# One group of zeros a pass in place of two, masks ahead of pooled scores, and a product moved into the pooled scores' buffer

## The chip, the cores and the metric

The kernel runs on one core of one Trainium2 chip. Its time is the device time of one execution in microseconds; the kernel before took 652.89 us as the median of three runs (650.90 to 655.39). One execution of it was profiled.

## The reference

Attention over 2 batches of 8 heads, 576 tokens, head size 64, followed by two feed-forward networks. The attention has two parts that are added: a local one, in which a token sees the three tokens on either side, and a pooled one over means of four tokens.

```python
def sm_attn(qq, kk, vv):
    s = scale * np.matmul(qq, kk.transpose(0, 1, 3, 2))
    s = s - np.max(s, axis=-1, keepdims=True)
    a = np.exp(s)
    a = a / (np.sum(a, axis=-1, keepdims=True) + 1e-09)
    return np.matmul(a, vv)
q_d = q.reshape(B, H, Sd, factor, D).mean(axis=3)      # k_d, v_d likewise, factor = 4
out_up = np.repeat(sm_attn(q_d, k_d, v_d), factor, axis=2)
mask = np.abs(pos[:, None] - pos[None, :]) < factor
scores = np.where(mask, scale * np.matmul(q, k.transpose(0, 1, 3, 2)), -1000000000.0)
# softmax of scores, times v: out_local
return (out_up + out_local).astype(np.float32)
```

The result x (1152 tokens of 512 numbers) goes through h = x w_in, g = h clip(h + 3, 0, 6) / 6, g w_out, and then through four experts, max(x w1, 0) w2, weighted by normalised probabilities and added.

## The kernel before

The attention runs in units of two heads (one batch, one pair of heads): eight units, numbered by `units`. A loop over t (lines 1116 to 1177, a pass below) works on three units at once: pass t makes the scores of unit t, transposes the probabilities of unit t - 1 and multiplies those of unit t - 2 with the values. Passes 8 and 9 only finish, and in between they already work on the first pieces of the next network (`pieces`, `first`, products L382 to L384). After the loop comes that network, then the experts.

In every pass from 2 to 7 TensorE gets, in this order: pooled scores (`pooled_scores`, L728) with four products of zeros ahead of them (`idle_products`, L605, 128 x 128 by 128 x 512, bf16), masks (`masks`, L652) and scores (`scores`, L665), transposes (`turn`, L712) with four more zeros ahead, values (`values`, L802) and pooled values (L813, in the same function), and pooled transposes (`pooled_turn`, L782). The products of zeros go into the buffer that the next real products overwrite. Pass 1 has the first four zeros only, pass 8 has neither.

The order on all five engines is that of the program's text; waits follow from the use of tiles. In a pass VectorE takes: maximum of the pooled scores (L741) and its scaling (L743), maximum of the scores (L682) and their subtraction (L683), the low half of an earlier result (L843), sums and reciprocals (L764 to L696), the adding up of both attentions (`xf`, L827), and one step of the conversion of the first network's weights (`convert`: L245, L255, L267, L276, L234). In passes 5 and 6 it also adds rows by fours for the pooled values of batch 1 (`add_four`, L452). ScalarE takes the exponentials (L753, L689), copies the transposes out (L719, L720, L790), copies pooled values (L821), writes the high half (L835) and steps of the conversion. GpSimd multiplies by the reciprocals (L769, L698) and sums q and k by fours for later units (`sums`, L452). Loads are issued by SyncE; some are held back by a one-element memset of VectorE (`hold`, L189).

Results of TensorE go into pairs of PSUM banks. `banks()` hands out three pairs in turn: each call takes the one that was handed out three calls earlier, and its first write waits for the last reader of that one. `banks(True)` hands out a fourth pair, on its own, for the values. `pool_last_v` (L485) multiplies the last 67 rows of v so that the last sixteen pooled keys of batch 1 come out; in the kernel before it uses the fourth pair at the end of pass 5's scores, and ScalarE copies the result out (L488).

Of the kernel before, what the change touches and what calls it, by code (L numbers as in the profile page):

```python
# [30 lines left out]
B, H, S, D = 2, 8, 576, 64  # L31
NHP = H // 2
# [31 lines left out]
NU = B * NHP  # L64
PK = S // FACTOR
KC = PK // 2


KR = ((80, 64), (P, PK - P))
# [56 lines left out]
def model(ctx: ExitStack, tc: tile.TileContext, qT, kT, v, dp, w_in, w_out, w1, w2, out):  # L126
# [15 lines left out]
    def banks(last=False):  # L142

        pool = psum["last"] if last and "last" in psum else psum["pair"]
        return pool.tile([P, 2, 512], F32, tag="pair", name="pair")
# [19 lines left out]
    def give(slot):  # L165
        unused[slot[1]] += 1
# [312 lines left out]
        for kc in range(2):  # L479
            nc.scalar.activation(out=pooled_v(0, kc), in_=pool[: KR[0][kc], kc, :], func=AF.Copy)  # L480

    def pool_last_v():

        to = banks(True)[: KR[1][1], 0, :]
        nc.tensor.matmul(  # L485
            to, last_fours, v_slots[1][NP - 1][0][:LAST_ROWS, :DM], start=True, stop=True
        )
        nc.scalar.activation(out=pooled_v(1, 1), in_=to, func=AF.Copy)  # L488
# [69 lines left out]
    for j in range(1, NJ):  # L558
        n = NI if j < 2 else NI - 1
# [43 lines left out]
    def idle_products(ps, count):  # L603
        for n in range(count):
            nc.tensor.matmul(ps[:, n % 2, :], zeros[:, :P], zeros, start=True, stop=True)  # L605

    class Unit:
# [91 lines left out]
                out=ex, in0=ex, in1=rec.unsqueeze(3).to_broadcast([QT, 2, NI, W]), op=ALU.mult  # L699
            )  # L700

        def turn(self, idle):

            tr = banks()
            idle_products(tr, idle)

            for p in range(NP):
                for h in range(2):
                    at = (2 * p + h) * HQ
                    for b in range(2 if p < NP - 1 else 1):  # L710
                        rows = slice(b * HQ, (b + 1) * HQ)
                        nc.tensor.transpose(  # L712
                            tr[:, b, at : at + HQ],
                            self.ex[rows, h, 2 * p : 2 * p + 2, :].rearrange("q r w -> q (r w)"),
                            ident[rows, rows],
                        )
            n = 2 * NP * HQ
            self.aT = att.tile([P, n + n - 2 * HQ], F32, tag="aT", name="aT", bufs=2)
            nc.scalar.activation(out=self.aT[:, :n], in_=tr[:, 0, :n], func=AF.Copy)  # L719
            nc.scalar.activation(out=self.aT[:, n:], in_=tr[:, 1, : n - 2 * HQ], func=AF.Copy)  # L720

        def pooled_scores(self, idle):
            self.sd = banks()
            idle_products(self.sd, idle)
            for qh in range(2):
                for h in range(2):
                    d = slice(h * D, (h + 1) * D)
                    nc.tensor.matmul(  # L728
                        self.sd[:KC, h, qh * PK : (qh + 1) * PK],
                        self.qd[d, qh * KC : (qh + 1) * KC],  # L730
                        self.kd[d],
# [41 lines left out]
                op=ALU.mult,  # L773
            )

        def pooled_turn(self):
            tr = banks()
            for h in range(2):
                for qh in range(2):
                    for kc in range(2):  # L780
                        c0 = kc * PK + qh * KC
                        nc.tensor.transpose(  # L782
                            tr[: self.kr[kc], h, c0 : c0 + KC],
                            self.exd[:, 2 * h + qh, kc * self.kr[0] : kc * self.kr[0] + self.kr[kc]],
                            ident[:KC, :KC],
                        )
            self.aTd = att.tile([P, 2, 2 * PK], F32, tag="aTd", name="aTd", bufs=2)
            for kc, n in enumerate(self.kr):
                part = slice(kc * PK, (kc + 1) * PK)
                nc.scalar.activation(out=self.aTd[:n, :, part], in_=tr[:n, :, part], func=AF.Copy)  # L790

        def values(self):
            b, hp = self.b, self.hp
            pv = banks(True)
            col = [(hp * 2 + h) * D for h in range(2)]
            for p, j, r in sorted((i // 2, j, i % 2) for i, j, _ in WINDOWS):
                c0 = p * QT + j * QB
                keys = slice(r * WP, r * WP + W)
                for h in range(2):
                    at = j * DM + col[h]  # L800
                    to = (j // 2 * 2 * NP + 2 * p + h) * HQ + j % 2 * QB
                    nc.tensor.matmul(  # L802
                        pv[h * D : (h + 1) * D, r, c0 : c0 + QB],
                        v_slots[b][p][0][keys, at : at + D],
                        self.aT[keys, to : to + QB],
                        start=True,
                        stop=True,
                    )
            toks = slice(b * S, (b + 1) * S)
            hi, lo = x[:, 0, hp, toks], x[:, 1, hp, toks]  # L810
            for kc in range(2):
                for h in range(2):
                    nc.tensor.matmul(  # L813
                        pv[h * D : (h + 1) * D, 0, NI * HQ : NI * HQ + PK],
                        pooled_v(b, kc)[:, col[h] : col[h] + D],
                        self.aTd[: self.kr[kc], h, kc * PK : (kc + 1) * PK],
                        start=(kc == 0),
                        stop=(kc == 1),
                    )
            pd = att.tile([P, 2 * KR[0][0]], F32, tag="pd", name="pd", bufs=1)  # L820
            nc.scalar.activation(out=pd[:, :PK], in_=pv[:, 0, NI * HQ : NI * HQ + PK], func=AF.Copy)  # L821
            xf = att.tile([P, NI * QT], F32, tag="xf", name="xf", bufs=2)
            self.xf = xf[:, :S]
            nj = 2 * QB // FACTOR
            for r in range(2):
                n = NI - r
                nc.vector.tensor_tensor(  # L827
                    out=xf.rearrange("p (a r j f) -> p a r j f", r=2, j=nj, f=FACTOR)[:, :n, r],
                    in0=pv[:, r, : n * 2 * QB].rearrange("p (a j f) -> p a j f", j=nj, f=FACTOR),
                    in1=pd.rearrange("p (a r j) -> p a r j", r=2, j=nj)[:, :n, r]  # L830
                    .unsqueeze(3)
                    .to_broadcast([P, n, nj, FACTOR]),
                    op=ALU.add,
                )
            nc.scalar.activation(out=hi, in_=self.xf, func=AF.Copy)  # L835
            self.hl = hi, lo
            if hp == NHP - 1:
                for s in v_slots[b]:
                    give(s)
# [238 lines left out]
    units = [Unit(u) for u in range(NU)]  # L1078
# [37 lines left out]
    for t in range(NU + 2):  # L1116
        if t == NU:
            psum.pop("last").release()
            psum["few"] = ctx.enter_context(
                tc.tile_pool(name="few", bufs=2, space=PSUM, side="right")  # L1120
            )
        if t < NU:
            n = units[t]
            if t == 0:
                n.masks(IDLE)
                n.scores()
                n.pooled_scores(0)
                n.less_max()
                units[1].sums()
                n.pooled_softmax()  # L1130
                n.normalise()
            else:
                n.pooled_scores(4)
                n.masks(0)
                n.scores()
                n.pooled_softmax()
                if t == 1:
                    units[0].pooled_normalise()
                    make_last_fours()
                    units[2].sums()  # L1140
                    load_qk(2)
                load_next(t)
                n.less_max()
        if t == NHP + 1:
            pool_last_v()
        if t == NHP + 2:
            add_four(1)
        if 2 < t < NU + 1:
            units[t - 3].low()
        if 0 < t < NU:  # L1150
            n.pooled_normalise()
            n.normalise()
            load_next(t)
        if 0 < t < NU - 2:
            units[t + 2].sums()
        if t == NU:
            pieces(1, banks()[:, 0, :TC])
        if t >= NU:
            units[t - 2].values()
        if t > NU:  # L1160
            pieces(1)
            units[t - 3].low()
            units[t - 2].low()
        if 1 <= t <= NU:
            units[t - 1].turn(0 if t in (1, NU) else 4)
        if 2 <= t < NU:
            units[t - 2].values()
        if t == 1:
            pool_v(8)
        if 1 <= t <= NU:  # L1170
            units[t - 1].pooled_turn()
        if t == NHP + 1:
            add_four(0)
        convert(3 if t >= NU else 2 if t == 3 else 1 if t > 3 else 0)
        load_next(t)
        if t >= NU:
            pieces(1)
# [130 lines left out]
    for r in range(NR):  # L1308
        h = [
            work["pool"].tile([P, 2, 2, NT], F32R, tag="h", name="h", bufs=2) for _ in range(2)  # L1310
        ]
# [85 lines left out]
```

## Time and profile before

| | |
|---|---|
| median of three runs | 652.89 us (650.90 to 655.39) |
| span of the profiled execution | 651.4 us (no time of its own is given beside it) |
| TensorE products busy | 642.8 us, 99% of the span |
| VectorE, ScalarE, GpSimd busy | 64%, 39%, 15% of the span |
| passes 2 to 7 | 19.64 to 66.03 us |

Times are microseconds from the start of the span. Shares over the whole span say little of the passes, which are its first tenth; the stages there are read from timelines and windows. An engine's row in the timeline tells its start, its length, the line, and in brackets how long the engine stood idle before it and what ended that.

### The profile page before, as it was taken

Reading aid. Unit: us, or ns where it says so; the run is one execution under the profiler, and the core shown is the slowest. Engines: PE = TensorE matmul, PEld = TensorE weight load, DVE = VectorE, ACT = ScalarE, POOL = GpSimd, SP = SyncE. Lnnn points to the kernel's source line nnn. Section 1 sums busy time; section 2 is a strip of 40 time slices with the busy share of each in tenths; the row PEclk is TensorE's granted clock in tenths of the full one; section 3 lists DMA queues with packets and bytes.
Section 4 is the critical chain, followed back from the end, with each engine's and each line's share of the span. In section 5 each row is a group of like instructions: output and inputs, shape, how many; then the busy total and the mean of one; then the engine's idle time right before and its main releaser. Section 6 shows DMA issues by size and latency. Waiting matters only on the chain.

```text
span 651.4 us, 11939 instructions
## 1 busy us (share of the span) xinstructions
PE 642.8 (99%) x4909; PEld 581.5 (89%) x4909; DVE 417.8 (64%) x848; ACT 252.7 (39%) x590; POOL 95.8 (15%) x141
## 2 busy tenths in 40 slices
PE   7999999999999999999999999999999999999997
PEld 3556899999999999998898998998998998988986
DVE  6578799962596228595575665665665765765742
ACT  5566576542464235352232233233241341331310
POOL 4753100000000035200201201201201201201000
PEclk9988999999999999999999999999999999999999
DMA  8754424500330110300110110110110210300012
GB/s 260 243 175 148 187 84 138 186 1 1 130 130 0 65 65 1 130 2 1 65 65 0 66 65 0 65 65 2 64 65 1 87 45 0 130 1 1 2 49 97
DMA packets 13368, 46.97 MB, mean 72 GB/s; under 512 B 1385, under 2 KB 4457, under 8 KB 9602
## 3 DMA queue, kind: packets, MB, share of 16 engines
q1 hardware_dynamic: 13314, 46.21, 21.0%
q8 instruction: 38, 0.62, 0.4%
q14 instruction: 16, 0.13, 0.1%
HBM read 43.85 MB, written 2.36 MB: 71 GB/s over the span
## 4 chain that ended last, share of the span: by engine, by line
PE 95%; DMA 2%; DVE 1%; SPq 1%; ACT 0%; issue 0%; POOL 0%; ACTq 0%; POOLq 0%
PE bank L994 27%; PE bank L382 10%; PE bank L383 10%; PE bank L384 10%; PE bank L1273 10%; PE bank L1274 10%; PE bank L1275 10%; PE pair L802 2%; PE pair L605 2%; DMA slot<-in_qT_dram 1%; PE pair L813 1%; DMA slot<-in_v_dram 1%; PE pair L728 1%; PE pair L782 1%; PE pair L665 1%; PE pair L712 0%
## 5 line engine op out<-in xcount | busy, mean ns | idle before, releaser
L994 PEld LDWEIGHTS bank<-xop,slot 128*128 128x128 f32 x1344 | 180.0, 188 | 1.2
L994 PE MATMUL bank<-xop,slot 128*128 128x288 f32 x1344 | 180.8, 295 | 0.0
L1274 PE MATMUL bank<-slot,h 128*128 128x512 f32 x288 | 112.2, 390 | 0.0
L1273 PE MATMUL bank<-slot,h 128*128 128x512 f32 x288 | 112.1, 389 | 0.0
L1275 PE MATMUL bank<-slot,h 128*128 128x512 f32 x288 | 112.1, 389 | 0.0
L1281 DVE SCALAR_TENSOR_TENSOR slot<-bank,pr,slot 128x512 f32<-128x512 f32 x63 | 47.3, 750 | 80.7 <-PE bank L1275 80.7
L452 POOL TENSOR_TENSOR st<-slot 128x256 f32<-128x256 f32 x16 | 13.8, 862 | 462.0 <-DMA slot<-in_w_dram 232.0
L384 PE MATMUL bank<-h,slot 128*128 128x384 f32 x192 | 64.7, 337 | 0.0
L382 PE MATMUL bank<-h,slot 128*128 128x384 f32 x192 | 64.7, 337 | 0.0
L383 PE MATMUL bank<-h,slot 128*128 128x384 f32 x192 | 64.7, 337 | 0.0
L1275 PEld LDWEIGHTS bank<-slot,h 128*128 128x128 f32 x288 | 54.1, 188 | 11.4
L1273 PEld LDWEIGHTS bank<-slot,h 128*128 128x128 f32 x288 | 54.1, 188 | 10.7
L1274 PEld LDWEIGHTS bank<-slot,h 128*128 128x128 f32 x288 | 54.1, 188 | 10.6
L382 PE MATMUL bank<-x,slot 128*128 128x384 f32 x188 | 63.2, 336 | 0.0
L384 PE MATMUL bank<-x,slot 128*128 128x384 f32 x188 | 63.0, 335 | 0.0
L383 PE MATMUL bank<-x,slot 128*128 128x384 f32 x188 | 63.0, 335 | 0.0
L452 DVE TENSOR_TENSOR u<-bank,u 128x288 f32<-128x288 f32 x96 | 43.6, 454 | 20.4 <-PE bank L994 20.0
L1023 ACT ACTIVATE h<-c 128x288 fp32r<-128x288 f32 x64 | 27.7, 445 | 70.8 <-DVE c L452 70.8
L312 ACT ACTIVATE slot<-st 128x512 fp32r<-128x512 f32 x32 | 19.2, 624 | 63.0 <-POOL st L306 63.0
L883 DVE TENSOR_TENSOR h<-slot,h 128x384 fp32r<-128x384 f32 x48 | 27.0, 576 | 24.1 <-ACT h L882 24.0
L874 ACT ACTIVATE t<-bank,half__145 128x384 f32<-128x384 f32 x47 | 27.0, 580 | 38.7 <-PE bank L384 38.5
L875 DVE SCALAR_TENSOR_TENSOR slot<-t,bank 128x384 f32<-128x384 f32 x47 | 25.7, 551 | 24.3 <-ACT t L874 24.1
(121 smaller groups left out, 925.4 us busy)
## 6 DMA issues: line engine op xcount, KB each, us to landing
slot<-in_w_dram SPq DMA_DIRECT2D x16, 1024.0 KB, 4.9
slot<-in_w_out_dram SPq DMA_DIRECT2D x8, 1024.0 KB, 5.0
slot<-in_w_in_dram SPq DMA_DIRECT2D x5, 1024.0 KB, 5.9
slot<-in_v_dram SPq DMA_DIRECT2D x8, 512.0 KB, 5.5
slot<-in_w_in_dram SPq DMA_DIRECT2D x6, 512.0 KB, 4.4
out_dram<-slot SPq DMA_DIRECT2D x9, 256.0 KB, 2.0
slot<-in_kT_dram SPq DMA_DIRECT2D x3, 576.0 KB, 4.4
slot<-in_qT_dram SPq DMA_DIRECT2D x6, 288.0 KB, 5.0
```

The costliest lines, as they stand in the source:

```text
L382: nc.tensor.matmul(ps, wh, xh, start=first, stop=False)
L383: nc.tensor.matmul(ps, wh, xl, start=False, stop=False)
L384: nc.tensor.matmul(ps, wl, xh, start=False, stop=last)
L452: eng.tensor_tensor(out=out, in0=a, in1=b, op=ALU.add)
L874: nc.scalar.activation(out=t, in_=ps, func=AF.Relu, bias=half_, scale=1.0 / (6.0 * UP))
L883: nc.vector.tensor_tensor(out=g[:, 1, :], in0=u, in1=r32(g[:, 0, :]), op=ALU.subtract)
L994: nc.tensor.matmul(ps, a[:, i, k], b[:, j, k], start=start and k == 0 and n == 0, stop=stop and k == 1 and n == 2, skip_group_check=True,)
L1023: nc.scalar.activation(out=self.h[:, 0, i, j], in_=of, func=AF.Relu)
L1273: nc.tensor.matmul(ps, hh, w[:, 0], start=(f == 0), stop=False)
L1274: nc.tensor.matmul(ps, hh, w[:, 1], start=False, stop=False)
L1275: nc.tensor.matmul(ps, hl, w[:, 0], start=False, stop=(f == NF - 1))
L1281: nc.vector.scalar_tensor_tensor(out=to, in0=ps, scalar=share, in1=to, op0=ALU.mult, op1=ALU.add)
```

## The change

Masks and pooled scores change places at the head of a pass, and the four zeros ahead of the pooled scores and the four ahead of the transposes go. In passes 2 to 7, four zeros are issued between the values and the pooled values instead, into the pair that the pooled transposes use afterwards; for this `values` is split in two. The product for the last sixteen pooled keys moves from the end of pass 5 to pass 6, behind the pooled softmax, and writes rows 96 to 111 of the pooled scores' pair in place of the fourth pair.

```diff
@@ -64,6 +64,9 @@
 NU = B * NHP
 PK = S // FACTOR
 KC = PK // 2
+
+
+FREE = 96
 
 
 KR = ((80, 64), (P, PK - P))
@@ -479,9 +482,9 @@
         for kc in range(2):
             nc.scalar.activation(out=pooled_v(0, kc), in_=pool[: KR[0][kc], kc, :], func=AF.Copy)
 
-    def pool_last_v():
-
-        to = banks(True)[: KR[1][1], 0, :]
+    def pool_last_v(sd):
+
+        to = sd[FREE : FREE + KR[1][1], 0, :]
         nc.tensor.matmul(
             to, last_fours, v_slots[1][NP - 1][0][:LAST_ROWS, :DM], start=True, stop=True
         )
@@ -699,10 +702,9 @@
                 out=ex, in0=ex, in1=rec.unsqueeze(3).to_broadcast([QT, 2, NI, W]), op=ALU.mult
             )
 
-        def turn(self, idle):
+        def turn(self):
 
             tr = banks()
-            idle_products(tr, idle)
 
             for p in range(NP):
                 for h in range(2):
@@ -773,8 +775,8 @@
                 op=ALU.mult,
             )
 
-        def pooled_turn(self):
-            tr = banks()
+        def pooled_turn(self, tr=None):
+            tr = banks() if tr is None else tr
             for h in range(2):
                 for qh in range(2):
                     for kc in range(2):
@@ -806,6 +808,11 @@
                         start=True,
                         stop=True,
                     )
+            self.pv = pv
+
+        def pooled_values(self):
+            b, hp, pv = self.b, self.hp, self.pv
+            col = [(hp * 2 + h) * D for h in range(2)]
             toks = slice(b * S, (b + 1) * S)
             hi, lo = x[:, 0, hp, toks], x[:, 1, hp, toks]
             for kc in range(2):
@@ -1130,10 +1137,12 @@
                 n.pooled_softmax()
                 n.normalise()
             else:
-                n.pooled_scores(4)
                 n.masks(0)
+                n.pooled_scores(0)
                 n.scores()
                 n.pooled_softmax()
+                if t == NHP + 2:
+                    pool_last_v(n.sd)
                 if t == 1:
                     units[0].pooled_normalise()
                     make_last_fours()
@@ -1141,8 +1150,6 @@
                     load_qk(2)
                 load_next(t)
                 n.less_max()
-        if t == NHP + 1:
-            pool_last_v()
         if t == NHP + 2:
             add_four(1)
         if 2 < t < NU + 1:
@@ -1157,18 +1164,23 @@
             pieces(1, banks()[:, 0, :TC])
         if t >= NU:
             units[t - 2].values()
+            units[t - 2].pooled_values()
         if t > NU:
             pieces(1)
             units[t - 3].low()
             units[t - 2].low()
         if 1 <= t <= NU:
-            units[t - 1].turn(0 if t in (1, NU) else 4)
+            units[t - 1].turn()
+        tr = None
         if 2 <= t < NU:
             units[t - 2].values()
+            tr = banks()
+            idle_products(tr, 4)
+            units[t - 2].pooled_values()
         if t == 1:
             pool_v(8)
         if 1 <= t <= NU:
-            units[t - 1].pooled_turn()
+            units[t - 1].pooled_turn(tr)
         if t == NHP + 1:
             add_four(0)
         convert(3 if t >= NU else 2 if t == 3 else 1 if t > 3 else 0)
```

## Rows read from the trace of the kernel before

**Rows 1.** Page, part 4: shares of the chain that ended last, by engine.
```profile
PE 95%; DMA 2%; DVE 1%; SPq 1%; ACT 0%; issue 0%; POOL 0%; ACTq 0%; POOLq 0%
```

**Rows 2.** Timeline of TensorE (start, us, operation, count, idle before): L485, then pass 7.
```profile
45.00 1.02 PE L485 MATMUL pair<-slot,last_fours 67*16 67x512 f32 x2
...
59.30 1.03 PE L605 MATMUL pair<-zeros 128*128 128x512 bf16 x4
60.26 0.71 PE L728 MATMUL pair<-slot 64*72 64x144 f32 x8
60.91 0.34 PE L652 MATMUL pair<-mask,identb 128*128 128x190 bf16 x2
61.17 0.84 PE L665 MATMUL pair<-slot 64*32 64x38 f32 x72
61.95 1.04 PE L605 MATMUL pair<-zeros 128*128 128x512 bf16 x4
62.91 0.58 PE L712 MATMUL pair<-ident,ex 64*128 64x64 f32 x10
63.43 1.35 PE L802 MATMUL pair<-aT,slot 38*64 38x32 f32 x72
64.71 0.86 PE L813 MATMUL pair<-aTd,slot 128*64 128x144 f32 x8
65.50 0.72 PE L782 MATMUL pair<-ident,exd 72*128 72x72 f32 x8
```

**Rows 3.** Waits of TensorE, first 180 us: total, times, longest (us).
```profile
PE pair L472 <- DMA slot<-in_v_dram: 1.0, 1, 1.0
PE pair L802 <- ACT slot L488: 0.9, 1, 0.9
```

**Rows 4.** Windows: length, busy of PE, PEld, DVE, ACT, POOL; granted clock, DMA.
```profile
30.25:33.95 3.70, 3.35 (x98) 2.69 (x98) 1.88 (x7) 2.04 (x8) 2.28 (x3) 1.00 0.48 158
34.00:37.35 3.35, 3.35 (x17) 1.43 (x15) 2.55 (x6) 2.37 (x5) 2.10 (x6) 0.50 0.59 174
47.00:51.00 4.00, 3.14 (x98) 2.56 (x99) 1.62 (x7) 2.24 (x8) 2.83 (x4) 1.00 0.85 256
51.00:59.30 8.30, 8.30 (x191) 5.03 (x189) 7.92 (x21) 5.33 (x17) 2.10 (x4) 0.79 0.36 115
59.30:66.03 6.73, 6.73 (x192) 4.50 (x189) 6.15 (x17) 5.28 (x17) 2.41 (x3) 1.00 0.54 161
68.30:71.40 3.10, 3.10 (x99) 2.60 (x99) 1.13 (x4) 0.87 (x2) 0.00 (x0) 1.00 0.00 0
```

**Rows 5.** Timeline of VectorE, passes 4 to 7 (columns as in 2).
```profile
42.30 0.82 DVE L827 TENSOR_TENSOR xf<-pair,pd 128x320 f32<-128x320 f32 x2 [1.03 <-ACT pd L821]
...
46.28 0.55 DVE L683 TENSOR_TENSOR ex<-pair,mx 128x380 f32<-128x380 f32 x1
...
50.94 0.82 DVE L827 TENSOR_TENSOR xf<-pair,pd 128x320 f32<-128x320 f32 x2 [2.18 <-ACT pd L821]
...
54.52 0.75 DVE L741 TENSOR_REDUCE mxd<-pair 72x4 f32<-72x576 f32 x1
...
55.96 0.55 DVE L683 TENSOR_TENSOR ex<-pair,mx 128x380 f32<-128x380 f32 x1
...
59.28 0.49 DVE L827 TENSOR_TENSOR xf<-pair,pd 128x320 f32<-128x320 f32 x1
...
63.20 0.55 DVE L683 TENSOR_TENSOR ex<-pair,mx 128x380 f32<-128x380 f32 x1
...
65.47 0.22 DVE L696 RECIPROCAL rec<-sm 128x10 f32<-128x10 f32 x1
66.00 0.82 DVE L827 TENSOR_TENSOR xf<-pair,pd 128x320 f32<-128x320 f32 x2 [0.31 <-ACT pd L821]
```

**Rows 6.** Timeline of GpSimd: sums for the pooled scores of pass 2.
```profile
19.59 1.17 POOL L452 TENSOR_TENSOR slot<-slot 128x288 f32<-128x288 f32 x2 [0.28 <-DMA slot<-in_qT_dram]
```

**Rows 7.** Timeline of ScalarE: second exponential of head 0, pass 6.
```profile
55.96 0.36 ACT L753 ACTIVATE exd<-pair,nm 72x144 f32<-72x144 f32 x1
```

## The prediction

> **What bounds the kernel now.** I read the chain of work that ended last first: TensorE holds 95% of it [rows 1], so time is won only where TensorE's own line of work gets shorter. Then I read TensorE's timeline over one pass of the loop over t (pass 7, 59.30 to 66.03) [rows 2, 4]. Start to start, in order: first zeros 0.96, pooled scores 0.65, masks 0.26, scores 0.78, second zeros 0.96, transposes 0.52, values 1.28, pooled values 0.79, pooled transposes 0.53 (the rest of 6.73). No gap stands between them: TensorE fills the pass, and 1.92 us of it are products of zeros that nobody reads.
>
> Next the waits of TensorE [rows 3]: one of 0.9 us in front of the values (L802), for ScalarE's copy L488 of the last sixteen pooled values, and one of 1.0 us for a load of v in pass 1. Last the windows [rows 4]. The granted clock is 1.0 nearly everywhere, but it halves (2.4 to 1.2 GHz) at about 34.0 and again at 51.0. What TensorE did before each fall: transposes, values, pooled values and pooled transposes, with no zeros among them and a gap (0.35 idle in 30.25 to 33.95, 0.86 idle in 47.00 to 51.00). A stretch with the same kinds of products, without zeros and without a gap (68.30 to 71.40), was not followed by a fall. A pass with a fall took 8.30, one without 6.73: a fall costs 1.57.
>
> VectorE matters too, although it is off the chain. From the add L827 of one pass to the end of the subtraction L683 of the next it works without a gap (no row between them names idle time): 42.30 to 46.83 (4.53), 50.94 to 56.51 (5.57), 59.28 to 63.75 (4.47) [rows 5]. The difference between them is what lies behind L827: a conversion step of the first weights in each, and one add of four rows more in the 5.57.
>
> **The change part by part.** *Zeros.* Passes 1 to 7 lose the four ahead of the pooled scores, passes 2 to 7 those ahead of the transposes, and passes 2 to 7 get four between values and pooled values. Net 28 products, 0.24 each, 6.7 us if TensorE never waited. The four of pass 1 are worth nothing: behind them TensorE stands until a load of v lands [rows 3], which doesn't move. In pass 2 the pooled scores wait for GpSimd's sums, done at 19.59 + 1.17 = 20.76 [rows 6], with or without zeros ahead. So the saving begins there. The pure pass is 6.73 - 0.96 = 5.77.
>
> *Order of buffers.* The pairs rotate over three buffers. Before, the zeros of a pass reused the pooled scores' own predecessors, and pooled transposes took the buffer of this pass's pooled scores. With masks first, the pair into which the new zeros and the pooled transposes go is the one that held this pass's scores. It is free only when VectorE has read them for the last time: L683. That is a new wait in front of the four zeros, and behind them in TensorE's queue stand pooled values, pooled transposes, and the next pass's masks, pooled scores and scores. It closes a ring: L683 ends, zeros 0.96, pooled values start, and 1.29 later (64.71 to 66.00) L827 starts [rows 2, 5]; that is 2.25, taken as 2.3 with the semaphore; then the 4.5 to 5.6 above to the next L683. What VectorE does meanwhile (63.75 to the end of L696 at 65.69, 1.94) fits into the 2.3, but in pass 6 it has the second add of four rows there, and L683 to L827 took 2.77 (56.51 to 59.28). The ring is 6.8 to 8.0 us against TensorE's 5.77, wherever a conversion step lies in it.
>
> The times follow. Pass 2: pooled scores at 20.8, zeros at 20.8 + 0.65 + 0.78 + 0.52 + 1.28 = 24.03, L827 at 26.28, TensorE through at 26.31. Pass 3 has no conversion step ahead of it, TensorE sets it: zeros at 26.31 + 0.26 + 0.65 + 0.78 + 0.52 + 1.28 = 29.80, L827 at 32.05. Pass 4: L683 ends at 32.05 + 4.5 (an estimate from the two rows with one conversion step) = 36.55, L827 at 38.85. TensorE was there at 35.57: a wait of 1.0. Pass 5: 38.85 + 4.53 = 43.38, L827 at 45.68. Pass 6: 45.68 + 5.57 = 51.25, L827 at 54.02. Pass 7: 54.02 + 4.47 = 58.49, and TensorE ends the pass 0.96 + 0.79 + 0.53 later, at 60.8. Before, it was 66.03. That is 5.2; I let the gap of 0.35 in pass 3 stand, since no row names an instruction that ended it, so 4.9 us. From there on the instructions are the same in both kernels, and I carry the 4.9 to the end.
>
> *Last sixteen pooled keys.* The product L485 (1.0 us [rows 2]) moves from pass 5 to pass 6, into rows 96 to 111 of the pooled scores' buffer, and its wait of 0.9 ahead of L802 goes. Its own time lies in TensorE's wait of pass 6, so it is free, if it does not wait. Whether it does, no row shows: in program order it stands behind VectorE's maximum and ScalarE's exponentials, which read rows 0 to 71 of the same bank. Lower bound nothing. Upper bound: it waits for the second exponential, 1.80 behind the start of L741 (54.52 to 56.32) [rows 5, 7]. L741 then starts at 45.68 + 3.58 = 49.26, L485 runs from 51.06 to 52.1, transposes and values to 53.9, the zeros come 2.6 later than above, and L827 comes at 56.1 in place of 54.02: 2.1 us. I take nothing, since the rows written and read are disjoint, and keep 2.1 for the range. The Trainium skill (PSUM — Partial Sum Buffer, "PSUM bank collisions raise a hardware error") says that two engines collide only in one bank and one quadrant of 32 partitions, and calls guarding by bank the simple version; by quadrant the sum would stay as it is, by bank it would be 2.1 us more. No run here shows yet which of the two this program's waits follow.
>
> *The clock.* Fewer zeros can mean more falls. The profiled execution had two, 1.57 each, and these are in the 651.4; the 4.9 counts none afterwards. Afterwards a stretch without zeros lasts from pooled values to values, 4.8 us plus TensorE's wait of about 1.0, in six passes. It is longer than the stretches before both falls and has a gap as they had, but it holds pooled scores and scores too, which those had not. So between none and one a pass: 0 to 6 x 1.57 = 9.4 us. I take three, midway. Part of each hides in the wait of 1.0, if it slows masks to values, and none of it if it slows zeros and pooled values; I take 1.0 each, 3.0.
>
> Sum: 651.4 - 4.9 + 3.0 = 649.5 for an execution like the profiled one. Its span is the only time it has; the median of the runs shown, 652.89, is 1.5 above it, and I add that: **651.0**.
>
> **The rivals.** *L485 waits for the exponentials.* For it: program order. Against it: disjoint rows. 651.0 + 2.1 = 653.1.
>
> *Faster: the ring does not hold.* If VectorE's steps between L827 and L683 get out of the way and the clock does not fall, TensorE alone sets the passes: 26.31 + 5 x 5.77 + 1.0 = 56.2, that is 9.8 earlier than 66.03, 651.4 - 9.8 + 1.5 = 643.1. Against it: the three gapless stretches of VectorE.
>
> *Slower: the clock stays low.* Four zeros a pass may be too few to win the clock back, and each low stretch makes the next one likelier. A pass at a mean clock of 0.79 cost 1.57, so one that is low throughout costs about 1.57 x 0.50 / 0.21 = 3.7; six cost 22, of which up to 1.0 a pass hides: 664 to 670. It decides from seven falls on (659.4 - 646.5 - 1.5 = 11.4, over 1.57). For it: both falls came with zeros on either side and none between. Against it: in the passes behind both falls the clock came back (1.00 from 59.30 on) [rows 4].
>
> **How the numbers follow.** About 1% of 652.89 (6.5 us) is what a measurement of this kernel can tell from no change. Forecast without the wait of L485: 0.45, 648 to 655. With it: 0.32, 649 to 658. Both lie within 1%: 0.77. Faster rival 0.08. Slower rival 0.15. The range reaches from 647 (no fall, no wait: 651.4 - 4.9 + 1.5 = 648.0, and a little of the faster rival) to 661 (L485's wait and six falls, and the mildest part of the slower rival), and leaves out about 0.07 below and 0.12 above.
>
> **What would show it.** Right: zeros of passes 4 to 7 wait about 1 us for L683; the first piece (L382) starts between 60.8 and 66; no wait in front of L802; two to four falls. Wrong: no wait for L683 (faster rival); a clock below 0.75 over passes 2 to 7 (slower rival); 2 to 4 us of idle time in front of L485 (its wait). A load that VectorE's earlier adds of four rows would have to wait for would also break the sum: those loads are issued behind VectorE's own memsets and don't come earlier by themselves.

## The result: slower by 1.1%

| | before | after |
|---|---|---|
| median | 651.89 us (650.03 to 655.39, four runs) | 657.96 us (657.41 to 664.12, four runs) |
| profiled execution: span, granted clock | 651.4 us, 0.995 | 656.5 us, 0.984 |
| first piece of the next network begins (end of passes 2 to 7) | 66.03 us | 70.95 us |
| from there to the end of the span | 585.4 us | 585.6 us |

The ratio is 1.0112, interval 1.0080 to 1.0145. A ratio, here and in the table below, may leave out executions more than 1.5% above the kernel's fastest, so where times scatter it can lie below the ratio of the medians. Of the 5.1 us that the span grew, 4.9 lie ahead of the first piece; behind it the kernels take the same time to 0.2 us. So everything below is about passes 2 to 7.

Lines of after are two to eight numbers higher: zeros L608, masks L655, pooled scores L730, scores L668, transposes L714, values L804, pooled values L820, pooled transposes L784; the product for the last sixteen pooled keys is L488, its copy L491, the exponentials of the pooled scores L755; VectorE's maximum L743, subtraction L686, add L834.

The page of after, part 4, shares of the chain by engine (before: [rows 1]), shows that TensorE still sets the time:

```profile
PE 93%; DMA 2%; DVE 2%; POOL 1%; SPq 1%; issue 0%; ACT 0%; POOLq 0%; ACTq 0%; DVEq 0%
```

The longest wait of TensorE in the first 180 us, two for GpSimd and the shortest (total, times, longest), where before had [rows 3]:

```profile
PE pair L488 <- ACT exd L755: 5.4, 1, 5.4
PE pair L714 <- POOL ex L701: 1.5, 2, 1.0
...
PE pair L714 <- POOL slot L455: 0.8, 2, 0.4
...
PE pair L804 <- issue: 0.2, 1, 0.2
```

The wait of 0.9 us ahead of the values is gone, as meant. In its place the moved product waits 5.4 us for the exponentials of the pooled scores. TensorE's timeline shows what happened around it:

```profile
36.84 1.89 PE L608 MATMUL pair<-zeros 128*128 128x512 bf16 x4
...
45.37 1.04 PE L608 MATMUL pair<-zeros 128*128 128x512 bf16 x4
...
48.58 0.84 PE L668 MATMUL pair<-slot 64*32 64x38 f32 x72
54.81 1.89 PE L488 MATMUL pair<-slot,last_fours 67*16 67x512 f32 x2 [5.39 <-ACT exd L755]
56.63 0.90 PE L714 MATMUL pair<-ident,ex 64*128 64x64 f32 x10
57.46 2.34 PE L804 MATMUL pair<-aT,slot 38*64 38x32 f32 x72
59.74 1.89 PE L608 MATMUL pair<-zeros 128*128 128x512 bf16 x4
...
67.39 1.36 PE L804 MATMUL pair<-aT,slot 38*64 38x32 f32 x72
68.68 1.04 PE L608 MATMUL pair<-zeros 128*128 128x512 bf16 x4
...
70.95 0.42 PE L385 MATMUL pair<-x,slot 128*128 128x384 f32 x1
```

The same four zeros take 1.04 us in one pass and 1.89 in another, the same values 1.36 and 2.34: that is the clock. The windows (length; busy of PE, PEld, DVE, ACT, POOL; granted clock, DMA) put bounds on it:

```profile
36.65:43.40 6.75, 6.75 (x109) 3.85 (x106) 4.62 (x13) 3.27 (x11) 3.51 (x5) 0.50 0.69 200
44.00:53.65 9.65, 5.43 (x178) 3.79 (x175) 8.64 (x22) 5.78 (x20) 5.02 (x7) 1.00 0.57 170
53.70:67.30 13.60, 12.48 (x196) 7.68 (x196) 6.70 (x18) 6.05 (x19) 1.97 (x2) 0.50 0.24 76
67.35:70.95 3.60, 3.60 (x94) 2.47 (x93) 2.07 (x7) 2.28 (x10) 1.93 (x2) 1.00 0.48 150
```

TensorE ran at 1.2 GHz for 6.8 and then for 13.6 us; the second stretch begins inside the wait of L488, during which TensorE stood idle from 49.42 (48.58 + 0.84) to 54.81. In [rows 4] a fall had been over within one pass.

What L488 waited for is in ScalarE's timeline of pass 6: the fourth exponential, its accumulator read, then the copy L491 and the next unit of work.

```profile
54.30 0.37 ACT L755 ACTIVATE exd<-pair,nm 72x144 f32<-72x144 f32 x1
54.56 0.20 ACT L755 ACTIVATION_READ_ACCUMULATOR exd<-pair,nm 72x1 f32 x1
56.74 0.59 ACT L491 ACTIVATE slot<-pair 16x512 f32<-16x512 f32 x1 [1.98 <-PE pair L488]
57.24 0.51 ACT L692 ACTIVATE ex<-ex 128x380 f32<-128x380 f32 x1
```

L488 begins at 54.81, 0.05 behind the end of the last accumulator read (54.56 + 0.20). It writes rows 96 to 111 of the pair's first bank; the fourth exponential reads rows 0 to 71 of its second. So the wait covers more than the rows written and more than the bank. ScalarE's copy then stands ahead of the exponential of the scores, L692, and holds that back too.

### The profile page after: what moved, and what is told of

Its sections match the earlier page's. It is cut to its first block, busy times and chain, and to the rows that moved or that the text cites. A ratio compares the mean times of both kernels' runs of the same rounds, so it can differ in the third digit from the quotient of the medians.

```text
span 656.5 us, 11891 instructions
## 1 busy us (share of the span) xinstructions
PE 640.6 (98%) x4881; PEld 582.3 (89%) x4881; DVE 418.7 (64%) x848; ACT 253.0 (39%) x590; POOL 95.9 (15%) x141
## 4 chain that ended last, share of the span: by engine, by line
PE 93%; DMA 2%; DVE 2%; POOL 1%; SPq 1%; issue 0%; ACT 0%; POOLq 0%; ACTq 0%; DVEq 0%
PE bank L1001 27%; PE bank L385 10%; PE bank L387 10%; PE bank L386 10%; PE bank L1286 10%; PE bank L1287 10%; PE bank L1285 10%; PE pair L804 2%; DMA slot<-in_qT_dram 1%; PE pair L820 1%; PE pair L608 1%; DMA slot<-in_v_dram 1%; PE pair L714 1%; PE pair L784 1%; PE pair L730 0%
```

## The experiments

The kernels differ in the order of work, the buffer of the moved product and the number and place of the zeros alone; what zeros write nobody reads. "Half clock" below is, for one execution, 2 x (1 - granted clock) x span, that is the time TensorE would have spent at 1.2 GHz (the clock is on record to 0.001, so this number moves in steps of 1.3 us); the table gives the median over the executions of each kernel.

| kernel | median us | ratio to before [interval] | half clock us |
|---|---|---|---|
| before (114 executions beside the other runs) | 651.61 | | 3.9 |
| after | 657.96 | 1.0112 [1.0080, 1.0145] | 18.4 |
| no_move | 661.93 | 1.0141 [1.0099, 1.0183] | 35.6 |
| move_only | 658.94 | 1.0117 [1.0088, 1.0147] | 13.2 |
| early | 662.07 | 1.0102 [1.0061, 1.0143] | 30.4 |
| fill | 659.48 | 1.0121 [1.0072, 1.0170] | 24.3 |
| before_early | 652.10 | 0.9996 [0.9976, 1.0017] | 6.5 |
| early_8 | 654.87 | 1.0036 [1.0016, 1.0056] | 3.9 |
| early_one8 | 659.59 | 1.0106 [1.0077, 1.0136] | 15.1 |
| before_half | 652.17 | 1.0008 [0.9981, 1.0036] | 11.1 |
| early_22 | 657.62 | 1.0122 [1.0084, 1.0160] | 28.9 |
| early_0 | 653.56 | 1.0028 [1.0006, 1.0049] | 35.2 |
| before_22 | 650.67 | 0.9999 [0.9981, 1.0017] | 10.4 |
| ahead | 652.06 | 1.0022 [1.0002, 1.0042] | 6.5 |
| early_turn | 652.15 | 1.0000 [0.9975, 1.0024] | 13.0 |
| before_mid | 661.59 | 1.0091 [1.0054, 1.0129] | 31.0 |
| swap | 654.00 | 1.0026 [1.0004, 1.0047] | 6.5 |
| before_early_22 | 650.96 | 0.9974 [0.9956, 0.9991] | 12.3 |
| after_ahead | 669.03 | 1.0249 [1.0203, 1.0295] | 57.4 |
| after_ahead_turn | 656.68 | 1.0081 [1.0054, 1.0109] | 23.6 |

Fitted over the executions of one kernel, a microsecond at half clock goes with 0.40 us of time in before and 0.31 to 0.33 in after, no_move, early and before_mid; in early one pass at half clock takes 9.89 us where after at full clock takes 6.20 (23.86 to 30.06), of which 0.39 is a wait for GpSimd. Within a kernel, then, time largely follows the clock. Between kernels it does not follow the clock alone: early_0 has 35.2 us at half clock and takes 653.56, early_one8 has 15.1 and takes 659.59.

### The moved product: undone, alone, moved elsewhere

**no_move**: after, with the product back at the end of pass 5's scores and in the fourth pair.

```diff
-                if t == NHP + 2:
-                    pool_last_v(n.sd)
+        if t == NHP + 1:
+            pool_last_v()
```

> The changed kernel with one part undone: the product for the last sixteen pooled keys (L485 before, L488 after) and its copy go back to the end of pass 5 and into the fourth pair. Theory W (the wait): the changed kernel is slow because that product waits 5.4 us in pass 6 for ScalarE's exponentials and the clock then stays at half for 13.65 us; without it the time is 648 to 651, at or below the kernel before, and passes 2 to 7 end at 62 to 65 us. Theory Z (the zeros): half of the zeros lets the clock fall, wherever the product stands; then the time stays at 655 to 658 and three or more stretches at half the clock remain.

The wait is gone, the time isn't won back: 661.93, above the ranges of both theories. The window of the profiled execution shows why; the clock is down from 26.1 on, with hardly any idle time (PE 37.49 of 37.50):

```profile
26.10:63.60 37.50, 37.49 (x667) 24.79 (x670) 20.42 (x56) 16.80 (x54) 14.93 (x25) 0.50 0.49 143
```

**move_only**: before, with the product alone moved as the change does it; all eight zeros a pass stay.

> The kernel before with only the product for the last sixteen pooled keys moved to pass 6 and into the pooled scores' pair; all zeros and the order of masks and pooled scores as before. Theory W: the product waits 3 to 5 us for the exponentials and the clock falls behind the wait; 654 to 657, 2 to 5 above the kernel before. Theory Z: zeros on both sides keep the clock, the wait costs at most 2; 650 to 654.

The wait in its profile (L756 is the exponential there), and the window behind it:

```profile
PE pair L488 <- ACT exd L756: 4.5, 1, 4.5
```

```profile
54.70:68.30 13.60, 13.60 (x192) 7.55 (x191) 5.23 (x15) 5.25 (x15) 1.97 (x2) 0.50 0.15 46
```

The wait (4.5) and the 13.6 us at half clock behind it come with the move alone, and so does a loss of 1.17% (658.94, again above both ranges). That is the first cause. no_move says that there is a second one; since after, with both, loses 1.12%, the two don't add up.

**early**: after, with the product at the head of pass 6 and in the fourth pair, ahead of everything that it could wait for.

```diff
             else:
+                if t == NHP + 2:
+                    pool_last_v()
                 n.masks(0)
...
-                if t == NHP + 2:
-                    pool_last_v(n.sd)
```

> The changed kernel with the product for the last sixteen pooled keys at the head of pass 6, ahead of the masks, in the fourth pair, its copy ahead of the exponentials on ScalarE. Theory W: neither the 5.4 us wait nor the 0.9 us wait of the kernel before; 647 to 650, the lowest of these four. Theory Z: 655 to 658 as the changed kernel.

In the profiled execution (665.61 us) no wait of TensorE between 33 and 75 us is over 0.2 us, and the clock is down all the same, from 19.8 to 74.4; the window, and the zeros of two passes in TensorE's timeline:

```profile
19.90:74.30 54.40, 53.96 (x1010) 35.98 (x1007) 31.45 (x85) 24.91 (x83) 22.31 (x35) 0.50 0.48 145
```

```profile
35.23 1.89 PE L608 MATMUL pair<-zeros 128*128 128x512 bf16 x4
...
45.12 1.89 PE L608 MATMUL pair<-zeros 128*128 128x512 bf16 x4
```

**fill**: after, with twenty zeros into the fourth pair ahead of L488, so that TensorE is busy while it waits.

```diff
                 if t == NHP + 2:
+                    idle_products(banks(True), 20)
                     pool_last_v(n.sd)
```

> The changed kernel with 20 more products of zeros (4.8 us at the full clock) into the fourth pair ahead of the product for the last sixteen pooled keys, in the time in which TensorE stands still. It splits theory W: if the low clock behind the wait is the larger part of the loss, the stretch of 13.65 us at half the clock goes and the time falls to 652 to 655; if the wait itself is all of it, it stays at 656 to 659. Theory Z: falls in the other passes remain, 655 to 658.

The wait fell to 1.0 us in the profiled execution (673.23 us, in which the clock had first fallen at 24.6, long before L488); the median is 659.48, with 24.3 us at half clock. Covering the gap does not keep the clock up, so the gap is not all of it.

**before_early**: before, with the product at the head of pass 6 (ahead of its pooled scores, with the call at the end of pass 5 taken out).

> The kernel before with only the product for the last sixteen pooled keys (L485) and its copy moved from the end of pass 5 to the head of pass 6, still in the fourth pair. Both theories: the wait of 0.9 us ahead of the values goes, and with it at most one fall of the clock (1.6 us); 648 to 651, 0 to 2.5 below the kernel before.

0.9996, with no wait for the copy of the sixteen rows. Moving the product costs nothing where it stays in the fourth pair; the wait of 0.9 of [rows 3] was worth nothing measurable.

### The zeros: how many, and where

The next kernels change only the zeros (and, where named early, keep the product at the head of pass 6 so that its wait is out of play). They were meant to tell a theory of number (four a pass are too few) from one of order (masks ahead of pooled scores) and one of place (behind the values instead of ahead of the transposes).

**early_8**: early, with four more ahead of the transposes, so two groups of four.

```diff
-            units[t - 1].turn()
+            units[t - 1].turn(0 if t in (1, NU) else 4)
```

> The kernel early (changed order, product at the head of pass 6, four zeros behind the values) with the four zeros ahead of the transposes back, so eight a pass in two groups. Theory C (count: with four zeros a pass the clock, once down, stays down): stretches at half the clock are single ones of 3.4 us again, 649 to 653. Theory O (the new order, with zeros and pooled values behind VectorE's subtraction, lets the clock fall): stretches of 10 us and more remain, 655 to 670.

**early_one8**: early, with all eight in the one group behind the values.

```diff
-            idle_products(tr, 4)
+            idle_products(tr, 8)
```

> The kernel early with eight zeros in the one group behind the values. Theory C, by number alone: as early_8, 649 to 653. If the spacing of the groups matters (one group a pass leaves 4.8 us and more without zeros): falls remain, but each ends at the next group, 651 to 657. Theory O: 655 to 670.

**before_half**: before, without the four ahead of the pooled scores from pass 2 on; four ahead of the transposes stay.

```diff
-                n.pooled_scores(4)
+                n.pooled_scores(4 if t == 1 else 0)
```

> The kernel before without the four zeros ahead of the pooled scores in passes 2 to 7; its order, its four zeros ahead of the transposes and the place of L485 are untouched. It leaves 24 products of zeros out, nothing of the result. Theory C: stretches of 10 us and more at half the clock, 655 to 670, as early and no_move. Theory O: the order of before keeps the clock, and the zeros left out are time won: 645 to 650.

early_8 keeps the clock as before does (3.9 us at half) and still loses 0.36%. early_one8 with as many zeros has 15.1, and before_half with half as many 11.1, against 30.4 of early. So number alone does not decide, though eight zeros behind the values leave half of what four leave there. before_half missed both of its ranges (652.17). It also answers what the zeros are worth: 24 products, 5.8 us at 0.24 each, are gone, and the time is that of before. In its profiled execution (651.41 us) the passes end at 62.47, 3.6 us ahead of before's 66.03, and 1.4 of that is lost behind them (586.8 us to the end against 585.4). TensorE's waits in its profile say where much of the 5.8 went:

```profile
PE pair L802 <- ACT slot L488: 1.5, 1, 1.5
PE pair L605 <- ACT aTd L790: 1.5, 3, 1.0
...
PE bank L382 <- DVE slot L875: 1.2, 1, 1.2
```

**early_22** and **before_22**: two ahead of the transposes and two in the other place (behind the values in early, ahead of the pooled scores in before). **early_0**: early without any zeros in passes 2 to 7.

```diff
-                n.pooled_scores(4)
+                n.pooled_scores(4 if t == 1 else 2)
-            units[t - 1].turn(0 if t in (1, NU) else 4)
+            units[t - 1].turn(0 if t in (1, NU) else 2)
```

> The kernel early with its four zeros a pass split: two ahead of the transposes, two behind the values. Theory count (four a pass can't win the clock back): as early, 30 us and more at half the clock in the median, 657 to 663. Theory spacing (what counts is how long a stretch without zeros lasts): low time of 10 us or less, 650 to 654.

> The kernel before with two zeros in place of four at both places, passes 2 to 7; order and L485 untouched (24 products of zeros fewer, as in before_half). Theory spacing: low time 3 to 8 us, 648 to 651, at or below the kernel before. Theory count: low time as in before_half or more, 652 to 658.

> The kernel early without any zeros in passes 2 to 7 (24 products of zeros fewer, nothing of the result). Theory count: the clock is at half from pass 2 or 3 to the end of pass 7, 45 to 65 us, and with 0.35 us lost for each us at half, as the runs so far have it, 664 to 672. Theory spacing says the same. If zeros have nothing to do with the clock, low time is as in early and the time 1 to 4 us below it.

The lines are those of before_22. early_22 loses 1.2%, before_22 nothing; neither theory had both half clocks (28.9 and 10.4). early_0 came out far below what I had expected: 653.56, with about as long at half clock (35.2) as early with its four zeros (30.4). Those four cost 1.82 us a pass at half clock (35.23 to 37.05 in early), 11 us in six passes, and did not bring the clock back; without them the median is 8.5 us lower, and the ratio 1.0028 in place of 1.0102. So part of what the zeros behind the values cost is their own length on TensorE's line, and not the clock. early_one8 says the same beside early_turn, which comes below: their times at half clock are close (15.1 and 13.0), and early_one8, with 24 zeros more, takes 7.4 us longer.

**early_turn**: early, with its four zeros ahead of the transposes and none behind the values. **before_mid**: the order of before, the product as in before, and the four zeros behind the values alone. **swap**: before, masks and pooled scores exchanged, nothing else. The lines are, in this order, from `turn` and the loop of early_turn and from the loop of swap.

```diff
+            idle_products(tr, idle)
...
-            idle_products(tr, 4)
...
-                n.pooled_scores(4)
-                n.masks(0)
+                n.masks(4)
+                n.pooled_scores(0)
```

> The kernel early (masks ahead of pooled scores, last product at the head of pass 6) with its four zeros a pass ahead of the transposes, none behind the values. Theory place (what lets the clock fall is that the group stands behind the values): about 11 us at half the clock in the median as in before_half, 650 to 653. Theory order (masks ahead of pooled scores): about 30 us as in early, 657 to 663.

> The kernel before with its order and its L485, its only zeros in passes 2 to 7 the four between values and pooled values, as the change places them. Theory place: about 30 us at half the clock, 656 to 663. Theory order: about 11 us as in before_half, 650 to 654.

> The kernel before with masks and pooled scores changed round alone; eight zeros a pass, four ahead of the masks and four ahead of the transposes. Theory place: clock as in the kernel before, 4 us at half, 650 to 653. Theory order: 10 us and more at half, or TensorE waits that add 2 to 3 us, 653 to 657.

With four zeros a pass, place decides. Behind the values, they leave 30.4 us (masks first) and 31.0 (pooled scores first) at half clock, with times of 662.07 and 661.59 and ratios of 1.0102 and 1.0091; ahead of the transposes the same four leave 13.0 and 11.1, with 652.15 and 652.17 and ratios of 1.0000 and 1.0008. The clock is the larger part of it but not all: at the 0.31 and 0.33 us for each us at half clock fitted above, 17.4 and 19.9 us less at half are some 5 and 7 of the 9.9 and 9.4 us between the medians (an estimate). Windows of the two profiles (early_turn, then before_mid) show how this looks. In early_turn the clock falls too, but it comes back after a stretch; in before_mid it stays down to the end of the passes (70.65) and beyond:

```profile
24.50:41.50 17.00, 16.36 (x295) 10.84 (x290) 8.77 (x25) 8.00 (x26) 7.26 (x14) 0.50 0.56 172
41.50:51.80 10.30, 9.66 (x284) 6.87 (x282) 7.87 (x24) 6.25 (x23) 6.03 (x8) 1.00 0.69 202
```

```profile
44.80:75.50 30.70, 30.70 (x492) 21.42 (x488) 15.82 (x41) 12.87 (x40) 7.43 (x10) 0.50 0.27 85
```

The exchange of masks and pooled scores costs 0.26% in swap, which alone of the three fell into the range of the order theory. It seems to do so by waits rather than by the clock (6.5 us at half; from 18 us to the first piece TensorE is idle for 4.9 us in its profile and for 1.4 in that of before). Nothing can be seen of it between early_turn and before_half.

**before_early_22**: before_early with the 2 + 2 zeros of before_22.

> The kernel before with two zeros in place of four at both places and L485 at the head of pass 6. Both theories: the wait of the values for the copy L488 (1.9 us in before_22) goes; low time as in before_22, 10 us; 648 to 651, the lowest time so far if the two gains add.

0.9974, the only kernel whose interval lies below 1, by a little; one of nineteen, so I make no more of it than that it is not slower.

### The moved product again: ahead of the pooled softmax

**ahead**: move_only, with the product issued ahead of the pooled softmax; rows and pair as in the change.

```diff
                 n.scores()
+                if t == NHP + 2:
+                    pool_last_v(n.sd)
                 n.pooled_softmax()
-                if t == NHP + 2:
-                    pool_last_v(n.sd)
```

> The kernel move_only (before, with the last product in pass 6 and in rows 96 to 111 of the pooled scores' pair), but with the product ahead of the pooled softmax in program order. If waits follow the whole pair and not rows: TensorE no longer waits for the exponentials, VectorE's maximum L741 of pass 6 waits for the product instead (about 1 us after the scores), no low stretch of 13.65 us; 650 to 653. If waits follow rows, neither waits, and move_only's 4.5 us had another cause; 649 to 652 with no wait of L741 on the product.

The wait of 4.5 is gone, and 1.0022 is left of 1.0117: with the product in this pair, program order made the wait. VectorE's maximum (L744 here) has one in its place:

```profile
52.62 0.75 DVE L744 TENSOR_REDUCE mxd<-pair 72x4 f32<-72x576 f32 x1 [1.31 <-ACT slot L491]
```

The last two runs put this into the changed kernel. **after_ahead**: after with this edit. **after_ahead_turn**: after with this edit and the four zeros ahead of the transposes.

> The changed kernel with only L488 issued ahead of the pooled softmax, in the same rows of the same pair. The wait theory alone (the wait of 5.4 us and the low clock behind it are the whole difference): 651 to 653. The theory of two causes (the four zeros behind the values also leave the clock down, as in early and no_move): no wait of TensorE over 1.5 us in front of L488, some 25 to 35 us at half clock, 657 to 663.

> The changed kernel with L488 ahead of the pooled softmax and the four zeros ahead of the transposes in place of behind the values; masks first, one group of four and the pair stay as the change has them. The theory of two causes: no wait in front of L488, some 11 to 13 us at half clock as in before_half and early_turn, 650 to 654, within 0.4% of before. The rival that something else of the change costs (the exchange of masks and pooled scores, or fewer zeros in any place): 655 to 660.

Both missed: 669.03, the slowest of all, and 656.68 where I had expected before's time. The timelines of after_ahead (its profiled execution took 658.28 us, with 21 us at half clock; the other five had 34 to 61) show what went wrong; ScalarE:

```profile
51.46 0.63 ACT L232 ACTIVATE slot<-slot 128x512 fp32r<-128x512 f32 x1 [0.15 <-DVE slot L192]
52.11 0.59 ACT L491 ACTIVATE slot<-pair 16x512 f32<-16x512 f32 x1
```

VectorE:

```profile
52.74 0.75 DVE L743 TENSOR_REDUCE mxd<-pair 72x4 f32<-72x576 f32 x1 [1.31 <-ACT slot L491]
...
54.18 0.55 DVE L686 TENSOR_TENSOR ex<-pair,mx 128x380 f32<-128x380 f32 x1
```

TensorE:

```profile
54.79 1.89 PE L608 MATMUL pair<-zeros 128*128 128x512 bf16 x4 [2.97 <-DVE ex L686]
```

In this order it is the maximum of the pooled scores that waits for the copy of the sixteen rows, and the copy stands on ScalarE behind a conversion step (L232). VectorE stands for 1.3 us, L686 comes later with it, and the zeros wait 3.0 us for L686 to free their pair: the ring of the prediction. The clock falls inside that wait, at 52.9, and stays down until 73.4. In after_ahead_turn the pooled transposes wait 1.4 for L686 in the same way, and the clock falls there too, at 55.6. In ahead the same maximum waits as long (1.31) and the pooled transposes 0.9, with 0.22% lost. So in this kernel the product costs time in the pooled scores' pair in either order. Of the kernels run, what undoes the loss is the product in the fourth pair together with the zeros ahead of the transposes (early_turn, 1.0000).

## Why the prediction was wrong, point by point

**The forecast.** 651.0 and "no change" against 657.96 and 1.0112. The range (647 to 661) held the time, with its upper end made for this wait and six falls; the number that I gave had neither the wait nor long stretches.

**Where the sum failed.** The forecast had the passes end at 60.8; they ended at 70.95. The 10.15 us between them are three terms.

- *L686 of pass 6 ends 2.9 late* (54.14, forecast 51.25). The add of pass 5 (L834) starts at 47.62 in place of 45.68, because TensorE was at half clock from 36.6 to 43.4; and from there to L743 VectorE took 4.53 in place of 3.58 [rows 5] with the same instructions, L270 among them at 0.88 us. VectorE in after:

```profile
47.62 0.82 DVE L834 TENSOR_TENSOR xf<-pair,pd 128x320 f32<-128x320 f32 x2 [0.63 <-ACT pd L828]
48.36 1.62 DVE L455 TENSOR_TENSOR slot<-slot 128x512 f32<-128x512 f32 x2
49.91 0.88 DVE L270 TENSOR_SCALAR slot<-slot 128x1024 uint16<-128x1024 uint16 x1
50.82 1.40 DVE L279 TENSOR_TENSOR slot<-slot 128x512 f32<-128x512 f32 x2
52.15 0.75 DVE L743 TENSOR_REDUCE mxd<-pair 72x4 f32<-72x576 f32 x1
...
53.59 0.55 DVE L686 TENSOR_TENSOR ex<-pair,mx 128x380 f32<-128x380 f32 x1
```

In before the same step (L267) took 0.41 us. GpSimd's sums ended just ahead of it there, and in after they ran beside it. GpSimd and VectorE in before, then GpSimd in after:

```profile
49.98 2.67 POOL L452 TENSOR_TENSOR slot<-slot 128x288 f32<-128x288 f32 x4
```

```profile
52.85 0.41 DVE L267 TENSOR_SCALAR slot<-slot 128x1024 uint16<-128x1024 uint16 x1
```

```profile
48.20 2.87 POOL L455 TENSOR_TENSOR slot<-slot 128x288 f32<-128x288 f32 x4
```

- *The wait of L488: 3.4.* From 54.81, product, transposes and values take 0.96 + 0.52 + 1.28 = 2.76 at full clock, so the zeros could have started at 57.57, not at 54.14.
- *Half clock from 53.7 to 67.35: 3.9.* Zeros at 59.74 instead of 57.57 (2.2), and from there to the values of pass 7 7.65 instead of 4.49 (3.2); 1.5 of it would have been a wait for L686 in the forecast.

The sum had allowed 3.0 for the clock and 0.35 for a gap, and 0.2 came behind the passes: 10.15 - 3.35 + 0.2 = 7.0, which is 656.5 against the 649.5 forecast for the execution.

**"I take nothing, since the rows written and read are disjoint."** Wrong, and this step by itself is enough for the loss: move_only, with nothing else changed, lost 1.17%. It is not the only step that failed, since no_move, with this one undone, lost 1.41%. The bound beside it, 2.1, was too small as well: it let the product wait for the second exponential, and it waited for the fourth; and it priced the wait without a fall of the clock, which came with it. The Trainium skill's rule (PSUM — Partial Sum Buffer, "PSUM bank collisions raise a hardware error"), that engines collide only in one bank and one quadrant, says what the hardware would bear, and no run here tests it. The program's waits were coarser than quadrants and than banks: L488 waited for a reader of other rows in the other bank of the pair.

**The clock.** Three falls of 1.0 us were a guess midway between none and six; what came were stretches of 6.8 and 13.6 us, 20 us at half clock in the profiled execution, 18.4 as the median over after's four. Two falls are fewer than three: what failed is the price, a fall that is over within a pass. What came lies towards the slower rival, the clock that stays low, which I had given 0.15, without its own sign: the mean granted clock from 18.85 to 70.95 was 0.80, not below 0.75. (That rival's sum holds a slip: 11.4 over 1.57 is 7.3, so it decides from eight falls on, not seven.) Its reason was at most half of it: I had it decided by how few zeros there are, and four ahead of the transposes lose nothing. In [rows 4] the clock came back in the passes of before, with zeros in before's places, and I carried that over to zeros in another place, for which there was no row.

**The wait for L686 (1.0 in passes 4 to 7).** Not seen in after: TensorE, at half clock or behind a wait for GpSimd, came later than L686 did (in pass 4 zeros at 36.84, L686 done at 36.69):

```profile
36.14 0.55 DVE L686 TENSOR_TENSOR ex<-pair,mx 128x380 f32<-128x380 f32 x1
```

The ring is real, though: 0.4 and 3.0 us in after_ahead.

**The gain.** Most of the 6.7 us of zeros was not there to be won: before_half left out 5.8 of them and its time is before's. Waits took part of it, and 7.2 us more at half clock another part, some 2.9 us at the 0.40 fitted for before (an estimate). What it would be with the clock at full throughout no run shows.

**What was right.** The copy's wait ahead of the values goes; nothing changes behind the passes; the time is decided by TensorE's line of work between 20 us and the first piece; and idle time in front of L485 was named as the sign of its wait.

**What stays open.** Why zeros behind the values hold the clock worse than the same zeros ahead of the transposes no run shows; the runs show that they do, in both orders of masks and pooled scores. Nor do they show how the two causes, each over 1% alone, come to 1.12% together in after.

## What to carry to other kernels

A product put into unused rows of a PSUM buffer can be tied to every reader of that buffer, in either order: take the wait for granted until a trace shows otherwise, and give such a product a buffer of its own. Idle products that keep TensorE's clock have two prices, the time at half clock and their own length, and only the time of a run adds them up: the same four cost 1% in one place and nothing in another, at half clock they themselves take twice as long, and early without any of them was faster than with four in the wrong place. And where TensorE works in a ring with VectorE and ScalarE, part of what is taken off it turns into waits.

## What the runs showed of the hardware that I had not expected

TensorE stayed at 1.2 GHz for 54.6 us (early, 19.8 to 74.4) while it was busy 53.96 of 54.40 us, and for 37.5 us in no_move with 37.49 busy: no idle time was needed for it to stay low. And one kernel's executions differ mostly by this: those of early run from 653.05 us, with 13.0 us at half clock, to 670.33, with 61.5.

One conversion step of VectorE (L267 or L270, 128 x 1024, uint16) took 0.41 or 0.42 us wherever GpSimd did nothing beside it, and 0.64 to 0.89 wherever GpSimd's sums ran, in the first 170 us of all twenty profiles.
